# A fused attention and expert kernel: first-token splits ahead of the branch, later splits of w_out, first-unit splits on VectorE

## The chip, the core and the metric

One core of a Trainium2 chip runs the whole program in one launch. The metric is the device time of one execution in microseconds (us). Five engines take part: TensorE (PE in the rows; PEld is its weight load), VectorE (DVE), ScalarE (ACT), GpSimd (POOL) and SyncE (SP, which issues most transfers). Each engine takes its own instructions strictly in program order and waits on semaphores for the others.

## What is computed

Cut to what matters, the reference is three stages, each fed by the one before:

```python
scores = scale * q @ k.T                       # (4, 8, 576, 576), head_dim 64
scores = where(scores >= max(scores) - tau, scores, -1e9)
x = softmax(scores) @ v                        # reshaped to 2304 tokens x 512
logits = x @ w_gate + modality_bias[modality_id]
e = argmax(logits, 1); gate = softmax(logits)[e]
x = gate * (relu(x @ w1[e]) @ w2[e])           # 8 experts, 512 -> 1024 -> 512
h = x @ w_in                                   # 512 -> 2048
out = maximum(0.01 * h, h) @ w_out             # 2048 -> 512
```

All inputs are float32. The kernel keeps the precision of float32 with TensorE's rounded type: a value is split into a high part h (a rounded copy, made by ScalarE) and a low part l = value - h (a subtraction), and each product is three matmuls: h·h, l·h and h·l. Weights are split in the same way, in pieces of 128x1024.

## The kernel before

**Attention** runs first and takes some 380 us; the change does not touch it. While it ends, the routing is computed (class Routing): the expert of each token, and tables that say which rows go to which unit.

**Units.** The expert stage works in units of 342 tokens of one expert. `NSTAT = 7` units are always there (the first is called `e`, then 0 to 5); more of them stand behind a branch in `extra` (L1427, `tc.If(nv[0] > u)`), which with these inputs skips them. A unit has 8 steps `g1` (first layer, one piece of 128 hidden columns each: 12 matmuls), then 8 steps `g2t` (second layer; d = 0 to 3, in two parts). Its own weights come as 8 pieces, each split by `wsplit` (L1109): ScalarE makes the high part (L1111), VectorE or, if `on_pool` is set, GpSimd the low part (L1112). A unit's rows are fetched by three indirect transfers from GpSimd (`unit_rows`, L1161), which can be issued when the routing table `tab` is there, and are turned by TensorE (`tr`, L1194).

**Order.** Nothing is scheduled automatically here. `step(pe, *fills)` (L1274) emits one step of TensorE, then the evacuation of the step before, then the fills that a table `fills[i]` holds for step i. In the first unit, the rest of the routing (`chain`, by the table `LATE`, L260) and the splits of its own weight pieces 1 to 7 (by `S0`, L263) are such fills:

```python
for k, i in enumerate(S0):
    fills[i].append(lambda k=k: first_w.split(k % 4 != 2))
```

So pieces 1, 2, 4, 5 and 6 (`we_1l` and so on in the rows) are subtracted by GpSimd, pieces 3 and 7 by VectorE. Each split also lets SyncE issue a further weight load (`stream`). All of VectorE's routing work in these steps stands in one queue with the low parts `hl` of the hidden values.

**Third stage.** After the branch the 2304 tokens go through w_in and w_out in nine passes of 256 (loop over m, L1475). A pass has 16 steps `g1` (12 matmuls of 256 columns each; result in one of four PSUM banks, `ps_a`) and 16 steps `g2` (t = 0, 1 and c = 0 to 7; 6 matmuls of 512 columns each). `leaky` (L1169) takes a `g1` result out: ScalarE g, VectorE g, ScalarE high part, VectorE low part. The x of a pass is split by `tok_split` (L1356) into four high and four low pieces, ScalarE at L1359 and VectorE at L1360; for pass 0 this stands directly behind the branch. In pass 0, the last four pieces of w_in (`wi_4` to `wi_7`, at steps 1, 3, 5, 7) and the eight pieces of w_out (`wd_0` to `wd_7`) are still to be split; piece c of w_out is first used at step 16 + c:

```python
fills[4 + (3 * k) // 2].insert(0, lambda k=k: moe2_o.split(False))
```

This puts the w_out pieces at steps 4, 5, 7, 8, 10, 11, 13 and 14.

Of the kernel before, what the change touches and what calls it, by code (L numbers as in the profile page):

```python
# [915 lines left out]
def tile_main(tc, q, k, v, tau, mod, w_gate, bias, w1, w2, w_in, w_out, out):  # L916
# [7 lines left out]
    with ExitStack() as ctx:  # L924
        c = ctx.enter_context(tc.tile_pool(name="c", bufs=1))
# [159 lines left out]
        first_w = unit_weights("e", "ab", ei0[0:1, 0:1])  # L1085
# [13 lines left out]
        def wtile(nm, tag, dt=F32R):  # L1099
            return (x_tag[0] if tag == "n" else w_p).tile([P, 1024], dt, tag=f"w{tag}", name=nm, bufs=8)  # L1100
# [3 lines left out]
        def atile(nm):  # L1104
            if nm[0] == "x" and x_tag[0]:
                return x_tag[0].tile([P, 256], F32R, tag="x", name=nm, bufs=x_tag[1])
            return w_p.tile([P, UT], F32R, tag="act", name=nm, bufs=AB)
# [193 lines left out]
        moe2_o = Weights([(wd[n].rearrange("p (o f) -> p o f", o=1), 1) for n in range(8)], "wd", "ni")  # L1301
# [49 lines left out]
        def tok_load(m, pool, tag, n):  # L1351
            x = pool.tile([P, 2048 if tag == "cvr" else 1024], F32, tag=tag, name=f"x{m}", bufs=n)[:, 0:1024]
            nc.sync.dma_start(out=x.rearrange("p (c n) -> p c n", c=4), in_=yt[:, m * 256:(m + 1) * 256].rearrange("(c p) n -> p c n", p=P))
            return x

        def tok_split(ffn, x, cc):  # L1356
            h, l = (atile("x" + nm)[:, 0:256] for nm in "hl")
            src = x[:, cc * 256:(cc + 1) * 256]
            nc.scalar.activation(out=h, in_=src, func=AF.Copy)  # L1359
            V.tensor_tensor(out=l, in0=src, in1=h.bitcast(F32), op=ALU.subtract)  # L1360
            ffn.x.append((cc, h, l))

        for u in range(NSTAT):
            last = u + 1 == NSTAT
            w_nxt = None if last else wts[u + 1]
            fills = {i: [] for i in range(17)}
            tr_at = 8
            if u == 0:
                for k in range(1, CB):
                    fills[8 + 3 * k].append(convs[k].load)  # L1370
                for i, fs in LATE.items():
                    for part, a, b in fs:
                        fills[i].extend(chain[part][a:b] if isinstance(chain[part], list) else [chain[part]])
                for k, i in enumerate(S0):
                    fills[i].append(lambda k=k: first_w.split(k % 4 != 2))
                fills[LATE_ROWS].append(lambda: rows.update({1: unit_rows(0)}))
                tr_at = LATE_TR
            else:
                for k, i in enumerate(SB):
                    fills[i].append(lambda k=k: wts[u].split(False))  # L1380
                if last:
                    fills[HOTS[0]].append(pos_tiles)
                    for i, f in zip(HOTS, (lambda: pos_low(0), lambda: pos_low(1), pos_high, lambda: pos_values(0), lambda: pos_values(1))):
                        fills[i].append(f)
                    fills[HOTS[5]].append(lambda: step(pos_tables))
            if not last:
                for k, i in enumerate(SA):
                    fills[i].append(lambda k=k: w_nxt.split(False))
            if u:
                for ia, ib, ic, id in CONV.get(u, STG):  # L1390
                    if cv < 16:
                        c = convs[cv]
                        nx = convs[cv + CB] if cv + CB < 16 else None
                        fills[max(ia, 0)].append(c.a)
                        fills[ib].append(c.b)
                        fills[ic].append(c.c)
                        fills[id].append(c.d)
                        if nx:
                            fills[id + 1].append(nx.load)
                        cv += 1  # L1400
            if u + 2 < NSTAT:
                fills[tr_at + 3].append(lambda: rows.update({u + 2: unit_rows(u + 1)}))

            if last:
                for k in range(4):
                    fills[10 + 2 * k].append(lambda k=k: split_in(k))
                fills[8].append(lambda: first.append(tok_load(0, cv_p, "cvr", CB)))
                fills[8].append(lambda: nv.append(nc.values_load(ei[0:1, NMAX:NMAX + 1], min_val=0, max_val=NMAX)))
            steps = [lambda f=f: cur.g1(f) for f in range(8)] + [None] + [lambda d=d, part=part: cur.g2t(d, part) for d in range(4) for part in range(2)]
            nxt = None  # L1410
            for i, f in enumerate(steps):
                if f:
                    step(f)
                elif last:
                    settle()
                if i == tr_at and not last:
                    nxt = unit_ffn(u, w_nxt, rows[u + 1])
                    step(lambda: nxt.tr(0, ps_x))
                if i == tr_at + 2 and not last:
                    step(lambda: nxt.tr(1, ps_a, "a"))  # L1420
                for f in fills[i]:
                    f()
            cur = nxt
# [28 lines left out]
        extra(NSTAT - 1)  # L1452
        manual.enter_context(tc.manual_schedule())
        ctx.enter_context(manual)
        cur = Ffn(None, 256, lambda c: moe2_i[c], lambda c: moe2_o.out[c], leaky, None, 7)
        for cc in range(4):
            tok_split(cur, first[0], cc)
        st2.close()
        x_tag[:] = ctx.enter_context(tc.tile_pool(name="xp", bufs=1, reuse_waits="tile", side="right")), 24
        raw_tag_x = x_tag[0], "raw", 3  # L1460
# [14 lines left out]
        for m in range(9):  # L1475
            fills = {i: [] for i in range(32)}
            box = {}
            if m == 0:
                for k in range(4, 8):
                    fills[2 * k - 7].append(lambda k=k: split_in(k))  # L1480
                for k in range(8):
                    fills[1 + k if k < 3 else 4 + (3 * k - 9) // 2].append(lambda: moe2_o.load(raw_x))
                    fills[4 + (3 * k) // 2].insert(0, lambda k=k: moe2_o.split(False))
            if m < 8:
                box.update(n=tok_ffn(m + 1))
                fills[18].append(lambda: box.update(x=tok_load(m + 1, *raw_tag_x)))
                for cc in range(4):
                    fills[24 + 2 * cc].append(lambda cc=cc: tok_split(box["n"], box["x"], cc))
            for f in range(16):
                step(lambda f=f: cur.g1(f), *fills[f])  # L1490
            nxt = box.get("n")
            cur.gate = lambda t, m=m: pgate[:, 2 * m + t:2 * m + t + 1]
            for t in range(2):
                for c in range(8):
                    step(lambda t=t, c=c: cur.g2(t, c, 8), *fills[16 + 8 * t + c])
            cur = nxt
# [30 lines left out]
```

## Time and profile before

| | us |
|---|---|
| runs before | 1042.01, 1040.18, 1041.30 (median 1041.3) |
| profiled execution, own time | 1041.74 |
| its span, first to last instruction | 1040.0 |
| TensorE busy | 1000.6 (96%) |
| VectorE busy | 637.0 (61%) |
| ScalarE busy | 567.5 (55%) |
| GpSimd busy | 392.7 (38%) |

The profile is of one execution. Its page gives the busy time of each engine; finer views give stretches (windows), single instructions in order of time with the idle time before them and what ended it (timeline), and all instructions of one line. An engine's busy share over the whole span hides the places where it waits, so the stretches around the three edits are what to read. TensorE's clock has two levels, 1.2 and 2.4 GHz; the column PEclk is the granted share of the higher one in a stretch.

### The profile page before, as it was taken

The page shows a single profiled execution, that of the slowest core. Times are in us where ns is not written, and L with a number is a line of the kernel's source. Part 1 is how long each engine was busy: PE and PEld are TensorE (multiplying, and loading weights), DVE is VectorE, ACT ScalarE, POOL GpSimd, SP SyncE. Part 2 cuts the span into 40 slices and gives each one's busy share as a digit, 9 for nine tenths or more (in the row PEclk, how much of TensorE's full clock was granted, in tenths as well). Part 3 has the DMA queues.
Part 4 walks back from the last instruction along what each step waited for, and adds up shares of the span by engine and source line. Part 5 has one row for each costly group of instructions (what it writes and reads, how often), then busy time and mean ns, then how long its engine had stood idle before and what let it go on. Part 6 is the DMA issues. An engine that isn't in the chain of part 4 may idle for free. (4 is left out here: it accounts for less than half of the span.)

```text
span 1040.0 us, 18246 instructions
## 1 busy us (share of the span) xinstructions
PE 1000.6 (96%) x6710; PEld 912.2 (88%) x6710; DVE 637.0 (61%) x1413; ACT 567.5 (55%) x1199; POOL 392.7 (38%) x409
## 2 busy tenths in 40 slices
PE   7999999999999888899999989999999999999997
PEld 4798898988998678899999988898998989889895
DVE  6888888888888948588968767241332414233140
ACT  4888888888888424565657637242332413233140
POOL 6687877887787555245433210000000000000000
PEclk8999999999999999899999999999999999999999
DMA  4422233323513148688899624301010010000000
GB/s 132 117 59 60 63 103 97 79 60 84 138 48 71 61 119 298 189 262 265 271 308 330 219 71 147 107 12 41 1 42 31 11 41 2 21 11 11 11 11 21
DMA packets 90931, 104.63 MB, mean 101 GB/s; under 512 B 33765, under 2 KB 71141, under 8 KB 90833
## 3 DMA queue, kind: packets, MB, share of 16 engines
q1 hardware_dynamic: 81664, 88.84, 28.8%
q0 software_dynamic: 5136, 9.64, 2.9%
q10 hardware_dynamic: 4032, 4.90, 1.4%
q8 instruction: 54, 0.88, 0.4%
q14 instruction: 45, 0.36, 0.1%
HBM read 74.17 MB, written 19.85 MB: 90 GB/s over the span
## 5 line engine op out<-in xcount | busy, mean ns | idle before, releaser
L1468 POOL DMA_INDIRECT out<-yo,prow x18 | 17.3, 963 | 414.7 <-ACT yo L1249 414.7
L1172 DVE TENSOR_TENSOR g<-h,g 128x256 f32<-128x256 f32 x144 | 61.2, 425 | 167.7 <-ACT g L1171 167.7
L331 POOL TENSOR_TENSOR Pl<-rw,Ph 128x384 fp32r<-128x384 f32 x115 | 114.2, 1006 | 20.0 <-ACT Ph L326 16.1
L436 ACT ACTIVATE e<-s,mx 128x576 f32<-128x576 f32 x144 | 105.7, 745 | 26.5 <-DVE tb L432 14.4
L428 DVE TENSOR_REDUCE mx<-s 128x1 f32<-128x576 f32 x144 | 107.1, 752 | 19.9 <-PE s L423 17.8
L450 DVE SCALAR_TENSOR_TENSOR pp<-s,tb,e 128x576 f32<-128x576 f32 x128 | 104.2, 815 | 8.0 <-ACT e L436 4.9
L1171 ACT ACTIVATE g<-h 128x256 f32<-128x256 f32 x144 | 55.2, 383 | 98.3 <-PE h L1212 98.3
L1249 ACT ACTIVATE yo<-y,pgate 128x512 f32<-128x512 f32 x18 | 12.4, 688 | 170.0 <-PE y L1230 170.0
L469 PE MATMUL t<-ident,pp 128*128 128x128 f32 x576 | 90.1, 279 | 1.5 <-ACT rw L326 1.5
L423 PE MATMUL s<-kt,qt 128*128 128x288 f32 x256 | 80.5, 330 | 4.3 <-DVE pp L450 3.8
L493 POOL TENSOR_TENSOR Ph<-rw,zz 128x384 fp32r<-128x384 f32 x76 | 76.9, 1012 | 7.9 <-ACT rw L326 6.1
L563 PE MATMUL o<-Ph,hv 128*128 128x320 f32 (+3 forms) x237 | 76.0, 332 | 0.0
L423 PE MATMUL s<-k,qt 128*128 128x288 f32 x256 | 72.1, 296 | 0.0
L469 PEld LDWEIGHTS t<-ident,pp 128*128 128x128 f32 x576 | 67.7, 144 | 4.4 <-ACT rw L326 2.1
L564 PE MATMUL o<-Pl,hv 128*128 128x320 f32 (+3 forms) x237 | 68.7, 301 | 0.0
L1360 DVE TENSOR_TENSOR xl<-x,xh 128x256 fp32r<-128x256 f32 x36 | 12.9, 421 | 84.4 <-ACT xh L1359 84.4
L326 ACT ACTIVATE rw<-t 128x384 f32<-128x384 f32 x111 | 54.5, 493 | 10.2 <-PE t L469 7.0
L423 PEld LDWEIGHTS s<-kt,qt 128*128 128x128 f32 x256 | 48.4, 189 | 9.2 <-DVE pp L450 8.0
L563 PEld LDWEIGHTS o<-Ph,hv 128*128 128x128 f32 x237 | 45.3, 191 | 12.2 <-issue 11.9
L423 PEld LDWEIGHTS s<-k,qt 128*128 128x128 f32 x256 | 48.7, 190 | 0.0
L566 PE MATMUL o<-Pr,rv 128*64 128x256 f32 x186 | 47.1, 389 | 0.0
L564 PEld LDWEIGHTS o<-Pl,hv 128*128 128x128 f32 x237 | 45.6, 192 | 0.1
(574 smaller groups left out, 3315.4 us busy)
## 6 DMA issues: line engine op xcount, KB each, us to landing
k<-kt SPq DMA_DIRECT2D x30, 304.0 KB
cv<-in_moe_w_in SPq DMA_DIRECT2D x8, 1024.0 KB
cv<-in_moe_w_out SPq DMA_DIRECT2D x8, 1024.0 KB
yt<-yo ACTq DMA_DIRECT2D x28, 171.0 KB
x<-yt SPq DMA_DIRECT2D x9, 512.0 KB
rk<-in_k SPq DMA_DIRECT2D x16, 256.0 KB
rq<-in_q SPq DMA_DIRECT2D x16, 256.0 KB
rv<-in_v SPq DMA_DIRECT2D x16, 256.0 KB
```

The source lines that it names most:

```text
L326: A.activation(out=out, in_=in_, func=AF.Copy)
L331: fn.tensor_tensor(out=out, in0=a, in1=b.bitcast(F32), op=ALU.subtract)
L423: T.matmul(ps[:, j, 0:288], a, c, start=(m == 0), stop=(m == len(ops) - 1))
L428: V.tensor_reduce(out=mx, in_=get(g, f"s{s}"), op=ALU.min, axis=AX.XY)
L436: A.activation(out=e, in_=get(g, f"s{s}"), func=AF.Exp, bias=get(g, f"mx{s}"), scale=-1.0)
L450: V.scalar_tensor_tensor(out=p.rearrange("p (a b) -> p a b", a=2), in0=get(g, f"s{s}"), scalar=get(g, f"tb{s}"), in1=get(g, f"e{s}"), op0= ...
L469: T.transpose(ps[:, m * P:(m + 1) * P], p[:, o:o + P], ident)
L493: G.tensor_tensor(out=hi, in0=rw, in1=zz.rearrange("p (a b) -> p a b", a=3), op=ALU.add)
L563: T.matmul(ps[:, a:b], V2[:, vb, :], hi[:, n, a:b], start=(c == 4), stop=False)
L564: T.matmul(ps[:, a:b], V2[:, vb, :], lo[:, n, a:b], start=False, stop=(c == 3))
L1171: nc.scalar.activation(out=g, in_=ps, func=AF.Copy, scale=0.01)
L1172: V.tensor_tensor(out=g, in0=ps, in1=g, op=ALU.max)
```

## The change

There are three edits.

First unit: all seven splits in the loop over `S0` have their subtraction on VectorE; GpSimd's five go to VectorE's queue, at the same steps.

Branch: the split of x for pass 0 moves from behind the branch into the last unit's steps 12, 13, 15 and 16, and writes into two tiles `x0h`, `x0l` of 128x1024 (in slots that held the unsplit w_in pieces 0 and 1) instead of eight tiles.

w_out: the eight splits of pass 0 go to steps 6, 8, 10, 12, 14, 16, 18 and 20, and the loads of pieces 3 to 7, each of which takes the buffer of the piece three before it, to steps 6, 8, 10, 12 and 14.

```diff
-        def tok_split(ffn, x, cc):
-            h, l = (atile("x" + nm)[:, 0:256] for nm in "hl")
+        def tok_split(ffn, x, cc, to=None):
+            h, l = (t[:, cc * 256:(cc + 1) * 256] for t in to) if to else (atile("x" + nm)[:, 0:256] for nm in "hl")
...
                 for k, i in enumerate(S0):
-                    fills[i].append(lambda k=k: first_w.split(k % 4 != 2))
+                    fills[i].append(lambda k=k: first_w.split(False))
...
                 fills[8].append(lambda: first.append(tok_load(0, cv_p, "cvr", CB)))
+                fills[12].append(lambda: first.extend((tuple(wtile(f"x0{p}", "i") for p in "hl"), Ffn(None, 256, lambda c: moe2_i[c], lambda c: moe2_o.out[c], leaky, None, 7))))
+                for cc, i in enumerate((12, 13, 15, 16)):
+                    fills[i].append(lambda cc=cc: tok_split(first[2], first[0], cc, first[1]))
...
-        cur = Ffn(None, 256, lambda c: moe2_i[c], lambda c: moe2_o.out[c], leaky, None, 7)
-        for cc in range(4):
-            tok_split(cur, first[0], cc)
+        cur = first[2]
...
-                    fills[1 + k if k < 3 else 4 + (3 * k - 9) // 2].append(lambda: moe2_o.load(raw_x))
-                    fills[4 + (3 * k) // 2].insert(0, lambda k=k: moe2_o.split(False))
+                    fills[1 + k if k < 3 else 2 * k].append(lambda: moe2_o.load(raw_x))
+                    fills[6 + 2 * k].insert(0, lambda k=k: moe2_o.split(False))
```

The order of the instructions shows where each edit lands. On VectorE, in the first unit (`hib`, `Bm` and `A` are routing, `hl` a hidden value's low part, `we_5l` to `we_7l` weight pieces; + is new):

```order
 L876 SCALAR_TENSOR_TENSOR hib<-bs,sa 128x18
 L767 TENSOR_TENSOR Bm<-iob,lob 128x570
+L1112 TENSOR_TENSOR we_5l<-wer_5943,we_5h 128x1024
 L1167 SCALAR_TENSOR_TENSOR hl<-h,hh 128x342
 L878 TENSOR_TENSOR A<-io_78,hib 128x810
 L879 TENSOR_TENSOR A<-A,tokidx 128x225
+L1112 TENSOR_TENSOR we_6l<-wer_5998,we_6h 128x1024
 L1167 SCALAR_TENSOR_TENSOR hl<-h,hh 128x342
 L1112 TENSOR_TENSOR we_7l<-wer_6026,we_7h 128x1024
```

Pieces 5 and 6 now stand between routing instructions; pieces 1, 2 and 4 do so further up in the same way.

On TensorE, directly behind the branch, with the engines whose semaphores each matmul waits for, before:

```order
L1428 UNCONDITIONAL_BRANCH [waits PE_49] x9
L1212 MATMUL h<-xh,wi_0h 128x256 [waits DVE_49,Activation_49]
L1212 MATMUL h<-xh,wi_0l 128x256
L1212 MATMUL h<-xh,wi_0h 128x256 [waits Activation_49]
...
L1212 MATMUL h<-xl,wi_0h 128x256 [waits DVE_49] x4
```

and now:

```order
L1431 UNCONDITIONAL_BRANCH [waits PE_49] x9
L1212 MATMUL h<-x0h,wi_0h 128x256 [waits DVE_49,PE_49]
L1212 MATMUL h<-x0h,wi_0l 128x256
L1212 MATMUL h<-x0h,wi_0h 128x256
...
L1212 MATMUL h<-x0l,wi_0h 128x256 x4
```

The first matmul no longer waits for ScalarE; its wait for VectorE is left.

On VectorE in pass 0, from the first w_out piece on (`g`, `hl` are the evacuation), before:

```order
L1112 TENSOR_TENSOR wd_0l<-wdr_11895,wd_0h 128x1024
L1172 TENSOR_TENSOR g<-h,g 128x256
L1177 TENSOR_TENSOR hl<-g,hh 128x256
L1112 TENSOR_TENSOR wd_1l<-wdr_11917,wd_1h 128x1024
L1112 TENSOR_TENSOR wi_6l<-wi_7177,wi_6h 128x1024
```

and now:

```order
L1112 TENSOR_TENSOR wi_6l<-wi_7177,wi_6h 128x1024
L1172 TENSOR_TENSOR g<-h,g 128x256
L1177 TENSOR_TENSOR hl<-g,hh 128x256
L1112 TENSOR_TENSOR wd_0l<-wdr_11889,wd_0h 128x1024
L1172 TENSOR_TENSOR g<-h,g 128x256
L1177 TENSOR_TENSOR hl<-g,hh 128x256
L1112 TENSOR_TENSOR wi_7l<-wi_7241,wi_7h 128x1024
```

No two splits stand side by side any more, and five instead of eight w_out pieces stand ahead of step 16.

## Rows read from the trace of the kernel before

**Rows 1.** Windows: stretch, length, each engine's busy us (count), PEclk, DMA share, GB/s.
```profile
412.90:419.40 6.50, 1.13 (x6) 0.42 (x5) 0.00 (x0) 0.00 (x0) 0.00 (x0) 0.87 1.06 331
419.40:424.60 5.20, 5.19 (x19) 5.19 (x20) 2.16 (x3) 2.21 (x4) 0.00 (x0) 0.50 0.31 98
424.60:604.00 179.40, 177.14 (x1146) 176.13 (x1145) 144.72 (x159) 114.23 (x168) 74.99 (x47) 1.00 0.79 258
604.00:621.10 17.10, 16.14 (x113) 15.27 (x111) 12.27 (x18) 5.71 (x8) 0.00 (x0) 1.00 0.28 94
...
625.40:629.40 4.00, 4.00 (x20) 3.98 (x21) 1.82 (x5) 2.09 (x5) 0.00 (x0) 0.57 0.55 152
629.40:652.00 22.60, 21.50 (x175) 20.81 (x175) 20.10 (x35) 17.61 (x37) 0.00 (x0) 1.00 0.50 163
652.00:1035.00 383.00, 381.43 (x2401) 342.83 (x2399) 113.78 (x297) 114.41 (x313) 16.94 (x18) 1.00 0.07 23
```

**Rows 2.** Timeline, VectorE, first unit: start, us, instruction [idle before <-releaser].
```profile
390.73 0.52 DVE L1167 SCALAR_TENSOR_TENSOR hl<-h,hh 128x342 fp32r<-128x342 f32 x1 [1.80 <-ACT hh L1166]
...
391.98 1.22 DVE L1112 TENSOR_TENSOR we_3l<-wer,we_3h 128x1024 fp32r<-128x1024 f32 x1
...
393.80 2.24 DVE L871 TENSOR_TENSOR ub<-uc,un 128x8 f32<-128x8 f32 x1
...
396.52 2.11 DVE L874 TENSOR_TENSOR val<-oh,ub 128x144 f32<-128x144 bf16 x1
...
399.00 1.91 DVE L876 SCALAR_TENSOR_TENSOR hib<-bs,sa 128x18 f32<-128x18 f32 x1
...
401.93 0.99 DVE L878 TENSOR_TENSOR A<-io,hib 128x810 f16<-128x810 f32 x1
...
405.54 0.17 DVE L883 SCALAR_TENSOR_TENSOR more<-un,cnt 128x8 f32<-128x8 f32 x1
...
408.48 0.30 DVE L892 TENSOR_TENSOR val<-oh,cb 128x144 f32<-128x144 bf16 x1
```

**Rows 3.** Timeline, GpSimd, first unit.
```profile
393.61 2.40 POOL L1112 TENSOR_TENSOR we_4l<-wer,we_4h 128x1024 fp32r<-128x1024 f32 x1 [2.21 <-ACT we_4h L1111]
...
405.74 1.14 POOL L1050 DMA_INDIRECT xg<-x_dram,tab  x1 [3.87 <-DVE more L883]
```

**Rows 4.** Timeline, TensorE, end of the first unit.
```profile
402.97 1.08 PE L861 MATMUL tab<-A,Bm 128*114 128x45 f16 x18 [1.43 <-DVE A L878]
...
404.14 0.49 PE L1242 MATMUL y<-hl,we_6h 128*128 128x342 f32 x1
...
419.41 0.64 PE L1194 MATMUL xT<-ident,xg 114*128 114x114 f32 x2 [2.83 <-DMA xg<-x_dram,tab]
```

**Rows 5.** Instructions of line L1428, the branch: duration ns min/median/max, first and last start.
```profile
L1428 ACTq EVENT_SEMAPHORE  x2: 17/17/17, 624.7 to 624.7; - x2
...
L1428 DVEq COMPARE_BRANCH  x1: 72/72/72, 620.1 to 620.1; - x1
...
L1428 DVEq EVENT_SEMAPHORE  x1: 21/21/21, 623.2 to 623.2; - x1
```

**Rows 6.** Timeline, TensorE, pass 0 of the third stage.
```profile
625.38 0.39 PE L1212 MATMUL h<-xh,wi_0h 128*128 128x256 f32 x1 [4.29 <-ACT xh L1359]
...
629.96 0.28 PE L1212 MATMUL h<-xh,wi_1h 128*128 128x256 f32 x1
...
638.44 0.28 PE L1212 MATMUL h<-xh,wi_4h 128*128 128x256 f32 x1
...
643.73 0.39 PE L1212 MATMUL h<-xh,wi_5h 128*128 128x256 f32 x1 [0.89 <-DVE g L1172]
...
651.87 0.40 PE L1228 MATMUL y<-wd_0h,hh 128*128 128x512 f32 x1
```

**Rows 7.** Timeline, VectorE, pass 0: one evacuation's two instructions.
```profile
634.39 0.42 DVE L1172 TENSOR_TENSOR g<-h,g 128x256 f32<-128x256 f32 x1
634.72 0.42 DVE L1177 TENSOR_TENSOR hl<-g,hh 128x256 fp32r<-128x256 f32 x1
```

## The prediction

> **What bounds the kernel now.** I read the windows view first. From 424.6 to 604 TensorE is busy in 177.1 of 179.4 us, and from 652 to 1035 in 381.4 of 383.0 [rows 1]: there it is the bound, so time won ahead of these stretches moves everything behind it forward, and time won on another engine inside them is worth nothing. That leaves three places where TensorE waits or runs slow, one for each edit.
>
> First unit: between 412.9 and 419.4 TensorE works 1.13 of 6.5 us, and in the next 5.2 us its clock is at the lower level (0.50) [rows 1]. It waits for the rows that unit 0 gathers; the last piece lands at 419.4 [rows 4]. GpSimd issues the first gather at 405.74, at once after VectorE's `more` (405.54) [rows 2, 3]. So the chain that sets the end here is VectorE's routing work, and behind it the landing.
>
> Branch: TensorE stands still for 4.29 us, until ScalarE has made the first high part of x (625.38) [rows 6], and the 4 us after that are mostly at the lower clock (0.57) [rows 1].
>
> Pass 0: from 629.96 (step 2 of 16) the steps come every (638.44 - 629.96) / 6 = 1.413 us. Fourteen steps should then take 19.8 us, but the first `y` is at 651.87, after 21.9 us [rows 6]. TensorE lost 2.1 us to waits for VectorE to empty a PSUM bank; the largest is 0.89 us [rows 6].
>
> **First unit, term A.** In VectorE's stretch before `more`, three tiny routing instructions take 2.24, 2.11 and 1.91 us (L871, L874, L876) [rows 2]. The second has the shape of L892, which takes 0.30 us [rows 2]; the other two handle fewer elements, and I give them 0.2 us each. The first ends at 396.04, and GpSimd's subtraction of `we_4l`, begun just before it, at 393.61 + 2.40 = 396.01 [rows 2, 3]. So they seem held until GpSimd is through. With the five subtractions gone from GpSimd this frees 2.04 + 1.81 + 1.71 = 5.6 us. The Trainium skill, page "SBUF — State Buffer", section "SBUF: two separate sides", says the same as a mechanism: VectorE and GpSimd share one pair of ports, locked for a whole instruction, and a VectorE operation with two inputs in SBUF is locked out by a GpSimd operation that reads SBUF, while transfers never slow an engine. By that rule the sum below stands; the opposite reading, that the busy transfers stretch these instructions, is the slower rival below, with its own price.
>
> Added to the same stretch are `we_4l`, `we_5l` and `we_6l`, each 1.22 us by `we_3l` [rows 2]: 3.7 us. `we_1l` and `we_2l` stand further up; VectorE idles 1.80 us before 390.73 [rows 2], which holds one, and the other replaces a stretch of the same kind. So `more`, and with it the gathers, come 5.6 - 3.7 = 1.9 us earlier. `A` (401.93) [rows 2] comes earlier too, and TensorE's wait of 1.43 us for it goes, with the slow matmuls (0.49 us each) behind it [rows 4], but that is worth nothing by itself: TensorE only reaches the wait for the gathers sooner. The weight loads that the splits trigger move forward with them, so the gathers meet the same traffic (1.06, that is all transfer engines busy [rows 1]). The landing may therefore move by anything from 0 (set by the traffic) to 2.5 us (the routing finishing still faster); I take 1.9, the row that is on the chain. The lower clock behind it stays: the idle time is not shorter.
>
> **Branch, term B.** The four high and four low parts move into the last unit's second half, where VectorE works 12.3 and ScalarE 5.7 of 17.1 us while TensorE works 16.1 [rows 1], so I cost them at nothing there. The load of x is issued at step 8, four steps ahead; if it were late, ScalarE's evacuation behind it would wait, and with it TensorE. What is late next? TensorE's first matmul still waits for VectorE, since the bank that it writes was last emptied by VectorE in the skipped body, and VectorE only signals for that body when it is through its own branch. It takes the branch at 620.1 and signals at 623.2, 3.1 us later [rows 5]. Two more subtractions now stand between its last weight split and its branch, but at 620.1 its sequencer ran ahead of the engine, so I give them 0.2 us: start at 623.4 instead of 625.4, B = 2.0. If the branch is instead taken after the last subtraction has begun, or if ScalarE's signal (624.7 [rows 5]) counts after all, TensorE starts near 624.8 and B = 0.6. The idle time falls from 4.3 to 2.3 us. Is it short enough to keep the clock? After a wait of 1.43 us the clock fell (matmuls of 0.49 us) [rows 4], after one of 0.89 us (643.73) the stretch stayed at 1.00 [rows 1, 6]. 2.3 us lies beyond the first, so I let the lower level stay. It costs now: two steps in 629.96 - 625.38 = 4.58 us instead of 2.83 [rows 6], 1.75 us.
>
> **Pass 0, term C.** VectorE's work in the 16 steps before: 32 evacuation instructions at 634.72 - 634.39 = 0.33 us [rows 7] is 10.6 us, and 4 + 8 splits at 1.22 us [rows 2] is 14.6: together 25.2 us, more than TensorE's 16 x 1.413 = 22.6. Now only 4 + 5 splits stand in these steps: 10.6 + 11.0 = 21.6 us, below 22.6, and no two side by side. Four banks let VectorE lag by some 4 x 1.4 us. So the 2.1 us of waits go. Pieces 5, 6 and 7 come at steps 16, 18 and 20 and are needed at 21, 22 and 23, three steps or more of about 1.4 us later, against about 2.3 us for a split on both engines. Each load still has six steps, 8.5 us, until its split; tokens of pass 1 are loaded at step 18 and split from 24, as before. C = 2.1, with 1.0 as its lower bound if half of the waits come back.
>
> **The sum** is against the profiled execution's own time, 1041.74 us, of which 1040.0 is the span; the 1.7 around it and the tail are untouched. 1.9 + 2.0 + 2.1 = 6.0 gives 1035.7 there. That execution lies 0.44 above the median of the runs, 1041.3, so the forecast for a median is **1035.3**.
>
> **Rivals.**
> 1. The clock stays up behind the branch, because the idle time is halved: 1.75 us more, 1033.5. For it: the wait of 1.43 us was followed by eighteen thin matmuls (`tab`, 1.08 us) [rows 4], so the light stretch there was longer than the wait alone. Against it: 2.3 us is about as long as both together.
> 2. The gathers' landing is set by the traffic, not by their issue: A = 0, 1037.2. For it: all transfer engines are busy from 412.9 to 419.4 [rows 1]. Against it: that traffic is started by the same splits and moves along.
> 3. TensorE leaves the branch only with ScalarE, or VectorE's branch is taken late: B = 0.6, 1036.7.
> 4. The w_out splits do not do what their spacing says: VectorE or the loads still lag, and the waits move into steps 16 to 23: C = 0, 1037.4.
> 5. Slower: transfers, not GpSimd, stretch VectorE's instructions in the first unit. Then nothing is freed, and the three splits in the chain take 2.2 us each like their neighbours: 6.6 us more before `more`, the gathers land 6.6 us later, and TensorE just waits. Less B and C, 4.1, that is 2.5 over the median: 1043.8. It turns slower than before when the chain grows by more than 4.1 us. Against it: `we_3l` took only 1.22 us in the same traffic [rows 2], and the long instructions end with GpSimd's.
>
> **How the numbers follow.** Chances: forecast 0.50; rival 1 0.20; rival 2 0.13; rival 3 0.08; rival 4 0.05; rival 5 0.04. The fastest end takes A 2.5, B 2.0 plus 1.75, C 2.1: 1041.3 - 8.4 = 1032.9; the slowest end without rival 5 takes A 0, B 0.6, C 2.1: 1038.6. The range is 1032.9 to 1038.6. About 0.2% (2.1 us) is what a measurement of this kernel tells from no change. Faster by more than that (below 1039.2) 0.91; within it 0.05, mostly two rivals at once; slower 0.04.
>
> **What would show it.** In the profile of the changed kernel: L871, L874 and L876 at 0.3 us or less and the first gather issued near 403.8; the last `xT` after a gather near 417.5. The first matmul of pass 0 some 2.3 us after the last one of unit 5, released by VectorE and not by ScalarE; behind it a stretch at the lower clock (or none: rival 1). The first `y` about 24.4 us after the first matmul of pass 0, with no idle of TensorE released by VectorE in between. Wrong would be: long routing instructions that remain with GpSimd idle (rival 5), a gather that takes longer from issue to landing (rival 2), or waits of `y` matmuls for `wd_5l` to `wd_7l` (rival 4).

## The result, and the profile after

| | before | after |
|---|---|---|
| median of the runs, us | 1041.65 (1040.18 to 1042.58, 4 runs) | 1033.72 (1031.61 to 1034.47, 4 runs) |
| ratio | | 0.9918, 95% interval 0.9901 to 0.9934 |
| profiled execution, its span, us | 1041.74, 1040.0 | 1031.61, 1029.7 |

By the ratio the change makes the kernel 8.5 us faster (6.9 to 10.3 by its interval); the two medians differ by 7.9. The forecast was 1035.3, a gain of 6.0; the time lies inside the range, 1.6 us below the forecast, and close to the 1033.5 of rival 1. The profiled execution is the fastest of the four, so its trace shows somewhat more than the median gained.

The windows of the kernel after, at the places of [rows 1] (stretch, length, busy us (count) of PE, PEld, DVE, ACT and POOL, PEclk, DMA share, GB/s):

```profile
409.40:416.00 6.60, 1.10 (x5) 0.49 (x4) 0.00 (x0) 0.00 (x0) 0.00 (x0) 0.79 1.05 323
416.00:420.00 4.00, 3.99 (x15) 3.99 (x16) 2.16 (x3) 1.75 (x3) 0.00 (x0) 0.50 0.50 181
...
616.20:618.30 2.10, 0.09 (x1) 0.00 (x0) 1.09 (x2) 0.46 (x1) 0.00 (x0) 1.00 0.30 94
618.30:622.30 4.00, 3.96 (x33) 3.99 (x34) 0.43 (x2) 1.36 (x3) 0.00 (x0) 1.00 0.12 16
622.30:641.40 19.10, 19.10 (x161) 19.10 (x161) 17.37 (x32) 14.90 (x33) 0.00 (x0) 1.00 0.48 164
```

The wait for the gathered rows is as long as before (6.6 us, all transfer engines busy), only earlier, and the lower clock follows it as before (0.50). At the branch TensorE stands still for 2.1 instead of 4.3 us, the stretch behind it is at the upper level (1.00, before 0.57), and pass 0 has no idle of TensorE any more (19.10 of 19.10 us).

First unit, VectorE, then GpSimd (start, us, instruction [idle before <-releaser]), to be held against [rows 2, 3]:

```profile
393.04 0.15 DVE L871 TENSOR_TENSOR ub<-uc,un 128x8 f32<-128x8 f32 x1
...
394.86 0.30 DVE L874 TENSOR_TENSOR val<-oh,ub 128x144 f32<-128x144 bf16 x1
...
395.53 0.18 DVE L876 SCALAR_TENSOR_TENSOR hib<-bs,sa 128x18 f32<-128x18 f32 x1
...
402.60 0.17 DVE L883 SCALAR_TENSOR_TENSOR more<-un,cnt 128x8 f32<-128x8 f32 x1
```

```profile
402.80 1.14 POOL L1050 DMA_INDIRECT xg<-x_dram,tab  x1 [12.92 <-DVE more L883]
```

The three routing instructions are back at 0.15 to 0.30 us. TensorE in the same execution, first unit and pass 0, to be held against [rows 4, 6]:

```profile
400.74 1.08 PE L861 MATMUL tab<-A,Bm 128*114 128x45 f16 x18
...
416.01 0.64 PE L1194 MATMUL xT<-ident,xg 114*128 114x114 f32 x2 [1.73 <-DMA xg<-x_dram,tab]
...
618.34 0.36 PE L1212 MATMUL h<-x0h,wi_0h 128*128 128x256 f32 x1 [2.05 <-DVEq L1431]
...
621.29 0.28 PE L1212 MATMUL h<-x0h,wi_1h 128*128 128x256 f32 x1
...
641.45 0.39 PE L1228 MATMUL y<-wd_0h,hh 128*128 128x512 f32 x1
```

And the branch (its line is now L1431), to be held against [rows 5]:

```profile
L1431 DVEq COMPARE_BRANCH  x1: 72/72/72, 615.3 to 615.3; - x1
...
L1431 DVEq EVENT_SEMAPHORE  x1: 21/21/21, 618.2 to 618.2; - x1
```

TensorE now starts 0.1 us after VectorE's signal, which comes 2.9 us after VectorE's branch.

Attention ends up to 3 us earlier or later from one execution to the next, so the first three columns below run from the first `rank` matmul of L741 (`rank<-oh,tri`; 387.93 in the trace of before, 387.28 in that of after). "Last rows turned" is the start of the last `xT` matmul that waits for gathered rows. All kernels of this study, each from its one profile, in us:

| kernel | first gather issued | last rows turned | unit 5 ends | wait at the branch | first two steps of pass 0 | third step to first `y` |
|---|---|---|---|---|---|---|
| before | 17.81 | 31.48 | 233.16 | 4.29 | 4.58 | 21.91 |
| after | 15.52 | 28.73 | 229.01 | 2.05 | 2.95 | 20.16 |
| e1_first | 15.54 | 28.65 | 229.96 | 4.62 | 5.15 | 21.89 |
| e2_branch | 17.91 | 30.96 | 232.14 | 2.12 | 4.44 | 21.91 |
| e3_wout | 18.17 | 31.64 | 232.82 | 4.73 | 5.29 | 19.82 |
| e4_after | 15.52 | 28.97 | 229.70 | 2.35 | 2.95 | 20.15 |
| e5_pool | 20.53 | 35.09 | 236.47 | 2.10 | 2.94 | 20.28 |
| e6_memset | 15.51 | 28.96 | 230.48 | 2.12 | 4.44 | 20.15 |
| e7_tab | 15.09 | 29.22 | 230.50 | 2.19 | 2.94 | 20.24 |
| e8_early | 15.52 | 29.68 | 230.41 | 2.12 | 4.43 | 20.15 |
| e9_layout | 15.51 | 29.17 | 230.70 | 2.10 | 4.39 | 20.16 |
| e10_memset2 | 15.64 | 28.80 | 231.01 | 2.10 | 2.95 | 20.16 |
| e11_early2 | 15.52 | 28.87 | 229.48 | 1.09 | 2.94 | 21.25 |
| e12_best | 13.97 | 28.18 | 227.96 | 0.71 | 2.95 | 20.19 |

The wait at the branch runs from the modelled end of TensorE's last matmul. Pass 0 has 16 steps: the first two take one piece of w_in (`wi_0`), the third begins with `wi_1` and the first `y` follows the sixteenth, so the last column is 14 steps.

### The profile page after: what moved, and what is told of

It reads as the page before. It is cut to its first block, busy times and chain, and to the rows that moved or that the text cites. A ratio compares the mean times of both kernels' runs of the same rounds, so it can differ in the third digit from the quotient of the medians.

```text
span 1029.7 us, 18242 instructions
## 1 busy us (share of the span) xinstructions
PE 997.0 (97%) x6706; PEld 908.5 (88%) x6710; DVE 635.3 (62%) x1418; ACT 567.3 (55%) x1199; POOL 380.7 (37%) x404
```

## Experiments

Four kernels ran on one chip against the same runs of before (median 1041.9 us).

**e1_first**: the first edit alone.

```diff
-                    fills[i].append(lambda k=k: first_w.split(k % 4 != 2))
+                    fills[i].append(lambda k=k: first_w.split(False))
```

> The kernel before with the first unit's five GpSimd subtractions moved to VectorE, nothing else. From the two traces (corrected for attention ending 0.6 us earlier in the one of after): the last gathered rows are turned 2.8 us earlier, the piece at the lower clock behind them is 0.5 us shorter, and units 0 to 5 wait 0.6 to 0.9 us less. Theory 'freed routing': 3.3 to 4.2 us faster than before. The prediction's term A would give 1.9 us. Rival 'landing set by the traffic': nothing, and the 3.3 us in the trace of after were chance or came from the other edits.

Measured: 1040.2 us, ratio 0.9973 (0.9961 to 0.9985), so 2.8 us faster (1.6 to 4.1). Its profile has the first gather at 15.54 and the last rows at 28.65, as in the changed kernel, while branch and pass 0 are those of before. The rival "landing set by the traffic" falls as it was stated (no gain); the gain is above the prediction's 1.9 and somewhat under the 3.3 to 4.2 read from the two traces. The next unit's weight loads (`w0r`) are issued 2.1 us earlier too (6.96 instead of 9.08 us after the `rank` matmul), so this run doesn't show which of the two the landing follows, the issue or a traffic that moved with it.

**e2_branch**: the second edit alone (the x tiles, the four splits in the last unit, `cur = first[2]`).

```diff
+                for cc, i in enumerate((12, 13, 15, 16)):
+                    fills[i].append(lambda cc=cc: tok_split(first[2], first[0], cc, first[1]))
...
-        for cc in range(4):
-            tok_split(cur, first[0], cc)
+        cur = first[2]
```

> The kernel before with the x split of pass 0 ahead of the branch, nothing else. If PE's wait behind the branch falls from 4.3 to 2.1 us and the clock falls behind it as in before: 2.2 us faster. If the clock stays up as in the one trace of after: 3.8 us. Rival: VectorE's 25.2 us of work in pass 0 are the bound while the w_out splits stand as before, so the 1.6 us that the clock gives are waited off again at the PSUM banks in pass 0, and only 2.2 us remain although the first matmuls run at 0.28 us.

Measured: 1040.2 us, ratio 0.9979 (0.9967 to 0.9991), 2.2 us faster (0.9 to 3.4). In its profile the wait at the branch is 2.12 us, but the clock fell behind it, and the wait of pass 0 for VectorE is left. TensorE's rows, then the window behind the branch:

```profile
622.52 0.35 PE L1212 MATMUL h<-x0h,wi_0h 128*128 128x256 f32 x1 [2.12 <-DVEq L1431]
...
640.74 0.38 PE L1212 MATMUL h<-x0h,wi_5h 128*128 128x256 f32 x1 [0.67 <-DVE g L1172]
```

```profile
622.50:626.50 4.00, 3.98 (x21) 4.00 (x22) 0.42 (x1) 1.27 (x2) 0.00 (x0) 0.57 0.18 31
```

That execution gives no verdict on the rival, since the clock gave nothing that could be waited off.

**e3_wout**: the third edit alone.

```diff
-                    fills[1 + k if k < 3 else 4 + (3 * k - 9) // 2].append(lambda: moe2_o.load(raw_x))
-                    fills[4 + (3 * k) // 2].insert(0, lambda k=k: moe2_o.split(False))
+                    fills[1 + k if k < 3 else 2 * k].append(lambda: moe2_o.load(raw_x))
+                    fills[6 + 2 * k].insert(0, lambda k=k: moe2_o.split(False))
```

> The kernel before with the w_out splits and loads of pass 0 at the new steps, nothing else. Term C: 2.1 us faster, no idle of TensorE released by VectorE from the first to the sixteenth step, first two steps still at the lower clock. Rival 'waits move to steps 16 to 23': no gain, y matmuls wait for wd_5l to wd_7l.

Measured: 1040.7 us, ratio 0.9981 (0.9967 to 0.9995), 2.0 us faster (0.5 to 3.4). TensorE's rows:

```profile
633.08 0.32 PE L1212 MATMUL h<-xh,wi_1h 128*128 128x256 f32 x1
...
652.90 0.39 PE L1228 MATMUL y<-wd_0h,hh 128*128 128x512 f32 x1
```

19.82 us for 14 steps, 2.1 less than before, and no idle of TensorE for VectorE or for a w_out piece between or behind them. Term C is what it was said to be.

**e4_after**: the changed kernel once more, on this chip.

> The changed kernel again. Sum of the parts by the prediction 6.0 us, by the trace of after 8 to 10. The question is the clock behind the branch: if the level stays up at a wait of 2.1 us in this execution too, its first matmuls of pass 0 take 0.28 us and the span is near 1030; if it fell here, they take 0.39 us and the span is near 1032 as in the other three executions of the changed kernel (1032.5, 1031.1, 1032.4).

Measured: 1035.1 us, ratio 0.9927 (0.9913 to 0.9941), 7.6 us faster (6.1 to 9.1). The three parts alone make 2.8 + 2.2 + 2.0 = 7.0: within the intervals they add up. The window behind the branch is at the upper level again, after a wait of 2.35 us:

```profile
620.80:624.80 4.00, 3.98 (x33) 4.00 (x34) 1.06 (x2) 1.91 (x4) 0.00 (x0) 1.00 0.18 31
```

The expectation that the executions near 1032 of span are those in which the clock fell was wrong: this one has a span of 1032.1 and did not lose it.

The next four ran together (before 1042.2 us). The first two ask what held VectorE.

**e5_pool**: the changed kernel, with five subtractions on GpSimd that nobody needs.

```diff
+                def first_split(k):
+                    first_w.split(False)
+                    if k % 4 != 2:
+                        h = first_w.out[-1][0].bitcast(F32)
...
+                        nc.gpsimd.tensor_tensor(out=dummy[0], in0=h, in1=h, op=ALU.subtract)
```

> The changed kernel, and beside each of the splits of we_1, we_2, we_4, we_5 and we_6 GpSimd also subtracts the high part from itself into a scratch tile that nobody reads (two inputs in SBUF, 128x1024). VectorE's instructions, their order and the weight loads stay. Theory 'held by GpSimd': VectorE instructions with two inputs that begin beside one of these five subtractions last until it ends, some 2.4 us, and `more` and the first gather come about 4 to 6 us later than in the changed kernel, counted from the first `rank` matmul (15.5 us there). Rival 'stretched by the transfers': the transfers are the same as in the changed kernel, so L871, L874 and L876 stay at 0.15 to 0.30 us and the gather does not move.

Measured: 1040.3 us, ratio 0.9985 (0.9974 to 0.9996), 1.6 us under before, where the changed kernel has 7.6 to 8.5. The first gather is issued at 20.53, 5.0 us later than in the changed kernel. GpSimd, then VectorE:

```profile
392.10 1.89 POOL L1380 TENSOR_TENSOR dum<-we_2h 128x1024 f32<-128x1024 f32 x1 [3.22 <-ACT we_2h L1111]
397.34 1.94 POOL L1380 TENSOR_TENSOR dum<-we_4h 128x1024 f32<-128x1024 f32 x1 [3.34 <-ACT we_4h L1111]
...
401.57 2.75 POOL L1380 TENSOR_TENSOR dum<-we_6h 128x1024 f32<-128x1024 f32 x1
```

```profile
392.12 1.91 DVE L758 TENSOR_SCALAR un<-q 128x8 f32<-128x8 f32 x1
...
397.86 1.44 DVE L764 SCALAR_TENSOR_TENSOR lob<-sa,rk 128x5 bf16<-128x5 f32 x1
...
402.49 0.50 DVE L1167 SCALAR_TENSOR_TENSOR hl<-h,hh 128x342 fp32r<-128x342 f32 x1
402.92 1.57 DVE L874 TENSOR_TENSOR val<-oh,ub 128x144 f32<-128x144 bf16 x1
```

Three small instructions that begin beside a subtraction of GpSimd end with it: 392.12 + 1.91 = 394.03 against 392.10 + 1.89 = 393.99; 399.30 against 399.28; 404.49 against 404.32. The kernel issues the same transfers as the changed kernel. So GpSimd holds VectorE, and rival 5 (stretched by the transfers) falls. The evacuation `hl` at 402.49, which has one of its two inputs in PSUM, is not held (0.50 us) although GpSimd is at work; L758 is, although it reads only one tile.

**e6_memset**: as e5_pool, but GpSimd fills the tile (`nc.gpsimd.memset(dummy[0], 0.0)`).

> As the run before, but GpSimd only fills the scratch tile with zeros five times: it writes 128x1024 and reads nothing in SBUF. If any work of GpSimd holds VectorE, instructions with two inputs are stretched here as well and the gather comes later than 15.5 us after the first `rank` matmul; if only reading does, they stay at 0.15 to 0.30 us and the gather stays at 15.5.

The fills wait for nothing, so all five ran ahead of their place, between 376 and 381 us. Two of them:

```profile
379.08 1.96 POOL L1380 MEMSET dum<- 128x1024 f32 x2
```

That is before the stretch that was to be tested; the run says nothing on the question and counts only as one more execution of the changed kernel (one run, 1037.3 us; gather at 15.51, clock fallen behind the branch).

**e10_memset2** (run later) puts a subtraction of 8 columns, which waits for the high part, ahead of each fill.

```diff
+                        nc.gpsimd.tensor_tensor(out=dummy[0][:, 0:8], in0=h[:, 0:8], in1=h[:, 0:8], op=ALU.subtract)
+                        nc.gpsimd.memset(dummy[0], 0.0)
```

> As the memset run, but each fill stands behind a tiny subtraction of 8 columns on GpSimd that waits for the high part, so that the five fills (1.96 us each there) now run beside VectorE's routing instructions. If any long work of GpSimd on SBUF holds VectorE: L764, L874 or we_4l last 1.4 to 2.9 us as beside the dummy subtractions, and the first gather comes some 4 to 5 us later than the 15.5 us after the first `rank` matmul of the changed kernel. If only reading two inputs does: they stay at 0.15, 0.30 and 1.22 us and the gather at 15.5 to 16.

GpSimd, then VectorE:

```profile
397.68 0.96 POOL L1381 MEMSET dum<- 128x1024 f32 x1
398.95 0.75 POOL L1380 TENSOR_TENSOR dum<-we_6h 128x8 f32<-128x8 f32 x1 [0.31 <-ACT we_6h L1111]
```

```profile
397.76 0.74 DVE L767 TENSOR_TENSOR Bm<-iob,lob 128x570 f16<-128x570 bf16 x1
398.43 1.22 DVE L1112 TENSOR_TENSOR we_5l<-wer,we_5h 128x1024 fp32r<-128x1024 f32 x1
```

One run took 1035.9 us, too few for a verdict on the time. Beside a fill of 0.96 us nothing is held: L767 (two inputs in SBUF) takes 0.74 us as ever, and the gather comes at 15.64. So, of the two kinds of GpSimd work tried, the one that reads SBUF holds VectorE and the one that only writes it does not. It works the other way too: the tiny subtraction, 0.20 to 0.23 us where no split runs beside it, takes 0.75 us beside VectorE's split (398.43 to 399.65) and ends at 399.70. This is what the Trainium skill, page "SBUF — State Buffer", section "SBUF: two separate sides", states of the pair of ports that VectorE and GpSimd share: whoever has it keeps it for its whole instruction, and a VectorE operation with two inputs in SBUF is shut out only by a GpSimd operation that reads SBUF. Here 1.44 and 1.57 us beside a reader, 0.74 beside a fill agree with it.

**e7_tab**: the changed kernel, with `tab`, `more` and the gathers one step earlier.

```diff
-... 9: ((3, 0, 0), (4, 0, 6), (5, 0, 0)),
+... 8: ((3, 0, 0), (4, 0, 6), (5, 0, 0)),
...
-LATE_ROWS, LATE_TR = 9, 13
+LATE_ROWS, LATE_TR = 8, 13
```

> The changed kernel with the routing's step 9 (the `tab` matmuls, `more` and the gathers) one step earlier, ahead of the first twelve y matmuls on TensorE: `tab` should begin when `A` is there, some 1.5 us earlier, and the first gather be issued 0.5 to 1.5 us earlier (we_7l and one evacuation still stand before it on VectorE). Theory 'the issue sets the landing': the last gathered rows come as much earlier, 28.8 us after the first `rank` matmul becomes 27.3 to 28.3, and the time falls by 0.5 to 1.5 us. Rival 'the traffic sets the landing': the rows land when they did, and the time is the same.

Measured: 1034.3 us, ratio 0.9931 (0.9915 to 0.9948), which can't be told from the changed kernel. The first gather came 0.43 us earlier (15.09), less than hoped since the split of we_7 still stood before it, and the last rows no earlier (29.22). GpSimd's third gather and TensorE's wait for it:

```profile
406.93 1.37 POOL L1050 DMA_INDIRECT xg<-x_dram,tab  x1 [0.30 <-issue]
```

```profile
418.19 0.64 PE L1194 MATMUL xT<-ident,xg 114*128 114x114 f32 x2 [1.35 <-DMA xg<-x_dram,tab]
```

The step is smaller than the spread of the landing (28.65 to 29.68 over the eight kernels with a gather at 15.5 to 15.6), so this doesn't decide whether the issue or the traffic sets the landing; e12_best takes it up.

**e8_early**: the changed kernel, with the x splits and two w_in splits earlier.

```diff
-                for k in range(4):
+                for k in range(2):
                     fills[10 + 2 * k].append(lambda k=k: split_in(k))
...
-                for cc, i in enumerate((12, 13, 15, 16)):
+                for cc, i in enumerate((12, 13, 13, 13)):
...
+                for k in (2, 3):
+                    fills[11 + k].append(lambda k=k: split_in(k))
```

> The changed kernel with the x splits of pass 0 at steps 12, 13, 13, 13 (instead of 12, 13, 15, 16) and the splits of w_in pieces 2 and 3 at steps 13 and 14 (instead of 14 and 16). Theory 'VectorE's branch sets the start of pass 0, and it is taken when VectorE's last wait for ScalarE ends': that wait ends some 2 us earlier, VectorE signals near 616 instead of 618.2, TensorE then leaves with its own branch, 0.7 to 0.9 us after its last matmul instead of 2.05: 1.2 us faster. Rival 'something else releases it': the idle stays at 2.0 to 2.4 us and the time is the same.

Measured: 1035.4 us, ratio 0.9942 (0.9925 to 0.9960), no faster than the changed kernel; the wait at the branch is 2.12. VectorE, then its branch (L1433 here):

```profile
616.40 1.23 DVE L1112 TENSOR_TENSOR wi_3l<-wi,wi_3h 128x1024 fp32r<-128x1024 f32 x1 [1.64 <-ACT wi_3h L1111]
...
617.84 0.38 DVE L1337 SCALAR_TENSOR_TENSOR pgate<-pgate,pos 128x18 f32<-128x18 f32 x2
```

```profile
L1433 DVEq COMPARE_BRANCH  x1: 72/72/72, 618.1 to 618.1; - x1
...
L1433 DVEq EVENT_SEMAPHORE  x1: 21/21/21, 621.0 to 621.0; - x1
```

My move had put the split of piece 3 ahead of the `pgate` instructions: it waited 1.64 us for ScalarE, `pgate` came last, and the branch was taken at 618.1, when the second of these two, which takes up the first one's result, had just been let go. In the traces of before and after the branch comes just as long after `pgate` begins (619.90 to 620.1, 615.10 to 615.3), with splits still queued behind it. So the branch does follow VectorE's last wait, but this kernel had not moved that wait against TensorE's last matmul.

**e11_early2** (before 1041.7 us): e8_early, with both w_in splits at step 13. The edit against e8_early:

```diff
-                    fills[11 + k].append(lambda k=k: split_in(k))
+                    fills[13].append(lambda k=k: split_in(k))
```

> The changed kernel with the x splits at steps 12, 13, 13, 13 and both splits of w_in pieces 2 and 3 at step 13. In the run with piece 3 at step 14, VectorE's wait for that piece's high part held the `pgate` instructions back and the branch was taken 0.9 us before TensorE's last matmul ended, as before. Theory 'VectorE takes its branch at its last wait': now that wait ends about 2.5 us before TensorE's last matmul, VectorE signals before TensorE is through, and TensorE leaves with its own branch, 0.6 to 0.9 us idle instead of 2.1: 1.3 us faster than the changed kernel, and 1.5 more where the clock then stays up. Rival: the idle stays at 2.0 to 2.4 us.

Measured: 1033.5 us, ratio 0.9921 (0.9901 to 0.9940). VectorE's `pgate` and the branch lines, then TensorE's start and ScalarE's first evacuation:

```profile
615.07 0.39 DVE L1337 SCALAR_TENSOR_TENSOR pgate<-pgate,pos 128x18 f32<-128x18 f32 x2
```

```profile
L1433 DVEq COMPARE_BRANCH  x1: 72/72/72, 615.3 to 615.3; - x1
L1433 DVEq EVENT_SEMAPHORE  x1: 21/21/21, 618.4 to 618.4; - x1
L1433 PEldq EVENT_SEMAPHORE  x1: 51/51/51, 618.8 to 618.8; - x1
L1433 ACTq COMPARE_BRANCH  x1: 58/58/58, 618.9 to 618.9; - x1
```

```profile
619.06 0.36 PE L1212 MATMUL h<-x0h,wi_0h 128*128 128x256 f32 x1 [1.09 <-PEq L1433]
```

```profile
622.91 0.38 ACT L1171 ACTIVATE g<-h 128x256 f32<-128x256 f32 x1 [4.45 <-SPq L1433]
```

Now VectorE signals (618.4) before TensorE is through its own branch (618.8): the wait falls to 1.09 us, and the releaser is TensorE's own queue. The mechanism of term B stands. But the microsecond is lost again in pass 0: the 14 steps take 21.25 instead of 20.16 us. ScalarE's first evacuation waits for SyncE and starts 3.9 us after TensorE's first matmul (2.6 us in the changed kernel, 620.93 - 618.34), so VectorE starts its evacuations that much later against TensorE and, with nine splits still in these steps, is the bound again. That evacuation does not move with TensorE's start: ScalarE takes its own branch 0.9 us after TensorE's last matmul here (617.97 to 618.9) as in the changed kernel (616.29 to 617.2), and the evacuation starts 4.9 and 4.6 us after that matmul.

**e12_best** (before 1041.0 us): e11_early2, with only four w_out splits ahead of step 16 and the w_out loads moved with them, and with e7_tab's edit and the split of we_7 behind the gathers. The lines that e11_early2 and e7_tab don't have:

```diff
-S0 = 0, 2, 3, 4, 5, 6, 7
+S0 = 0, 2, 3, 4, 5, 6, 8
...
-                    fills[1 + k if k < 3 else 2 * k].append(lambda: moe2_o.load(raw_x))
-                    fills[6 + 2 * k].insert(0, lambda k=k: moe2_o.split(False))
+                    fills[1 + k if k < 3 else (9, 11, 13, 15, 16, 17, 18, 19)[k - 3]].append(lambda: moe2_o.load(raw_x))
+                    fills[(9, 11, 13, 15, 16, 17, 18, 19)[k]].insert(0, lambda k=k: moe2_o.split(False))
```

> The kernel of the run before, with two more moves. First, the w_out splits at steps 9, 11, 13, 15, 16, 17, 18 and 19: only four of them stand ahead of step 16. There the 1.0 us that TensorE won at the branch came back as waits in steps 9 to 15, by my reading because VectorE, which starts only with ScalarE's first `g`, 3.9 us after TensorE's first matmul, is the bound again. If so, the stretch from the second step to the first `y` falls from 21.25 to 20.2 us; if ScalarE or the loads bound it, it stays, and y matmuls wait for wd_4l to wd_7l. Second, in the first unit the `tab` matmuls, `more` and the gathers one step earlier and the split of we_7 behind them: the first gather should be issued some 14 us after the first `rank` matmul instead of 15.5. If the issue sets the landing, the last gathered rows are turned at 27.3 instead of 28.9; if the traffic sets it, at 28.5 to 29, and the time from issue to landing grows to 14.5 or more. Time: 1031 if both hold, 1032.5 with the first alone, 1033.5 with neither.

Measured: 1034.4 us, ratio 0.9930 (0.9911 to 0.9951): no better than the changed kernel. TensorE, ScalarE, GpSimd, VectorE:

```profile
616.64 0.36 PE L1212 MATMUL h<-x0h,wi_0h 128*128 128x256 f32 x1 [0.71 <-PEq L1433]
...
649.84 0.50 PE L1229 MATMUL y<-wd_6l,xh 128*128 128x512 f32 x1 [0.77 <-DVE wd_6l L1112]
...
652.00 0.50 PE L1229 MATMUL y<-wd_7l,xh 128*128 128x512 f32 x1 [0.49 <-DVE wd_7l L1112]
```

```profile
647.47 1.06 ACT L1111 ACTIVATE wd_6h<-wdr 128x1024 fp32r<-128x1024 f32 x1 [1.88 <-DMA wdr<-wd]
```

```profile
405.22 2.10 POOL L1050 DMA_INDIRECT xg<-x_dram,tab  x1 [0.30 <-PE y L1243]
```

```profile
405.17 1.16 DVE L1112 TENSOR_TENSOR w_0l<-w0r,w_0h 128x1024 fp32r<-128x1024 f32 x1
...
406.91 0.40 DVE L894 TENSOR_TENSOR posi<-posf,rk 128x18 int32<-128x18 f32 x1
```

The first 16 steps are clean (20.19), which confirms VectorE as the bound in e11_early2. The price is what rival 4 of the prediction describes: the loads of pieces 6 and 7 are now issued at steps 15 and 16, three steps ahead of their splits instead of six, so ScalarE waits for them (1.88 us), TensorE waits for `wd_6l` and `wd_7l` (0.77 and 0.49 us), and from the first `y` to the first matmul of pass 1 it takes 664.43 - 639.78 = 24.65 instead of 663.79 - 641.45 = 22.34 us.

In the first unit the first gather comes 1.55 us earlier than in the changed kernel, but the third takes 2.10 us on GpSimd (1.23 there) and is through only 0.28 us earlier (407.32 - 387.97 = 19.35 against 406.91 - 387.28 = 19.63); the last rows come 0.55 us earlier. That fits a landing that follows the last issue rather than the first, but 0.55 us is less than the spread of the landing, so it is not shown; what is shown is that most of the earlier start was lost on GpSimd. The third gather begins while VectorE's `w_0l` runs (405.17 to 406.33), and VectorE's L894 (0.40 us, 0.18 in the changed kernel) ends at 407.31, with the gather (407.32). So the two engines seem to hold each other here as well; no run was made to test it.

## Why the prediction was right, point by point

**Step by step** (means over the profiles of the table, in us; the after column takes the kernels that have the edit and no further move at that place):

| term | forecast | measured |
|---|---|---|
| A, at the gather's issue | 1.9 | 17.96 to 15.53: 2.4 |
| A, at the end of unit 5 | 1.9 | 232.7 to 230.1: 2.6 |
| B, wait at the branch | 2.0 | 4.55 to 2.14: 2.4 |
| clock behind the branch | 0 (rival 1: 1.75) | 5.0 to 4.43 or 2.95: 0.6 or 2.1, mean 1.4 |
| C, pass 0 (with the new x tiles) | 2.1 | 21.90 to 20.19: 1.7 |
| sum, with A at the end of unit 5 | 6.0 | 8.1 (whole kernels: 8.5 and 7.6) |

**A** was right in mechanism and somewhat small. GpSimd's subtractions held the three routing instructions (e5_pool), and the landing came earlier with the issue (e1_first against rival 2, A = 0). Whether the issue sets it, or the weight loads that moved with it, stays open. The term that was mis-sized is the price of the three splits in the chain: I took 1.22 us each, but the next instruction starts 1.14 us after a split's start (`hl` at 394.44 in the trace of after, the split of `we_4` at 393.30), 3.4 in place of 3.7. In the two traces the stretch from L871 to `more` is 11.74 and 9.56 us, that is 2.2 shorter, as 5.6 - 3.4 says; the rest of the 2.4 lies ahead of L871 and in the spread between executions (17.81 to 18.17 without the edit). That TensorE's wait and the lower clock behind it would stay was right.

**B** was right: TensorE starts with VectorE's signal, 2.05 to 2.35 us after its last matmul (2.3 forecast), ScalarE plays no part, and rival 3 did not occur. VectorE's branch is taken at its last wait, with instructions still queued behind it, as the prediction read from [rows 5]. e11_early2 moved it by moving that wait; e8_early, which left the wait where it was against TensorE's work, left the branch there too. The wait before the change was larger in other executions (4.62, 4.73) than in the one profiled.

**The clock** is where the forecast fell short. The step that failed is the comparison of one wait with another: from a fall after 1.43 us and none after 0.89 us it concluded that 2.3 us must cost the clock. In nine profiles with a wait of 2.05 to 2.35 us the upper level stayed in five (the matmuls take 0.28 us, PEclk 1.00) and was lost in four (PEclk 0.57 to 0.59 over the first 4 us); with waits of 4.3 to 4.7 us it was lost in all three, with 0.71 and 1.09 us in neither of two. So forecast and rival 1 are both true, in different executions. Even where the level falls, the first two steps take 4.43 instead of 5.0 us. What decides it at about 2 us stays open: the wait's length does not (lost after 2.10, kept after 2.35).

**C** was right: 2.1 us with the old x tiles (e3_wout). Of these only 1.1 us is idle of TensorE in [rows 1] (22.60 - 21.50); the rest shows as longer steps and went with the same edit. Together with the second edit the gain is 1.7, because each step of pass 0 then takes 1.440 instead of 1.413 us, which the prediction did not have: 14 x 0.027 = 0.4 us.

**The slower rival** (rival 5) had its mechanism refuted by e5_pool: with the same transfers, VectorE's instructions were short without GpSimd's work beside them and long with it (L874: 0.30 and 1.57 us).

No version of these experiments beats the changed kernel beyond its interval: e11_early2 (1033.5) and e12_best (1034.4) each win a microsecond at one place and lose it at the next.

## What to carry to other kernels

A tiny VectorE instruction that lasts two microseconds and ends together with a GpSimd instruction is not slow, it is held; moving the GpSimd work onto VectorE can pay even where VectorE is the busier engine, since it pays 1.14 us per split for up to 2 us of hold. Before a branch, look for each engine's last semaphore wait: VectorE's branch was taken here when that wait ended, not when its work was done, and TensorE, which waited for VectorE's signal, started with it. A microsecond won for TensorE at the head of a stage is worth something only while the engines that empty its banks can follow; here ScalarE's first evacuation kept its place, and the microsecond was waited off in pass 0.

## What the runs showed of the hardware

- A step of twelve 256-column matmuls takes 1.440 us in pass 0 of every kernel with the new x tiles, where TensorE doesn't wait, and 1.413 us in passes 1 to 8 and in the kernels with the old tiles, at PEclk 1.00 in both. **e9_layout** asked whether the distance between h and l in the tiles matters.

```diff
-            h, l = (t[:, cc * 256:(cc + 1) * 256] for t in to) if to else ...
+            h, l = (to[cc // 2][:, j * 256:(j + 1) * 256] for j in (2 * (cc % 2), 2 * (cc % 2) + 1)) if to else ...
```

> The changed kernel with the high and the low parts of pass 0's x side by side: the first tile holds h and l of pieces 0 and 1, the second those of 2 and 3 (so a matmul pair reads 1 KB apart in a partition instead of two tiles apart). In the three runs with the new x tiles a step of pass 0 takes 1.440 us, in the two with the old ones 1.413. If the distance of h and l within the tiles matters, a step takes 1.413 us here; if it is the place of the tiles or something else, it stays at 1.440.

TensorE, the first matmul of the seventh and of the ninth step:

```profile
630.72 0.40 PE L1212 MATMUL h<-x0h,wi_3h 128*128 128x256 f32 x2
...
633.60 0.40 PE L1212 MATMUL h<-x0h,wi_4h 128*128 128x256 f32 x2
```

(633.60 - 630.72) / 2 = 1.44 (one run, 1035.3 us): it does not. Whether it is the place of the tiles is open.

- From an engine's branch to its next semaphore instruction it takes 2.9 to 3.1 us on VectorE (615.3 to 618.2) and 3.8 on TensorE (615.0 to 618.8 in e11_early2). The Trainium skill, page "Runtime: NRT & Kernel Launch", section "Instruction fetch mechanics", says that a taken branch out of the fetched pages has to fetch its target first. Between VectorE's branch and its signal, the traces of before, after, e8_early and e11_early2 have two or three packets of the instruction queues, against seven in the 90 us from 500 to 590 of after; which engine they were for, and whether the branch waited for them, no trace shows.
- The clock behind a wait of about 2 us differs from execution to execution with the same instructions around the branch: after and e6_memset waited 2.05 and 2.12 us and had 2.95 and 4.44 us for the same two steps.
